# Seven products of sums of quarters for the last four output projections of an attention and feed-forward kernel

## The chip, the cores and the metric

One Trainium2 chip, one of its cores. The metric is the device time of one execution in microseconds (us); lower is better. The kernel before was run 13 times: median 1199.19 us, lowest 1196.18, highest 1206.77.

## The reference

Two blocks, one after the other, all in float32. The first is an attention in which each query and key is assigned to one of 16 clusters and a query sees only the keys of its own cluster. The second multiplies the result (3072 tokens by 512) by a 512 x 2048 matrix, gates it elementwise, and multiplies it by a 2048 x 512 matrix:

```
q, k, v: (4, 8, 768, 64);  centroids: (8, 16, 64);  w_in: (512, 2048);  w_out: (2048, 512)
mask   = argmax cluster of q == argmax cluster of k
attn   = softmax(where(mask, q k^T / 8, -1e9)) v
x      = attn as (4*768, 8*64)
h      = x @ w_in
g      = h * erf(softplus(h))
out    = g @ w_out
```

The change concerns the last line alone, out = g @ w_out.

## The kernel before

**Tiling.** The attention works on 16 pairs of heads (NPAIR), each pair in 12 units (two halves of 384 queries by six tiles of 128 keys). The feed-forward part works on 12 chunks of 256 tokens (TB), three for each batch. For one chunk `hidden(n)` (line 599) makes g's first factor: 8 groups of 8 matmuls, each with a 128x128 block of w_in as weights and 256 tokens as the moving operand, into a PSUM tile `hp` of one bank; VectorE copies each group into `gs[n]`. The `hp` tiles come from `ps_x` (line 103), a pool of four buffers that the attention's `av` and `psum` tiles use too. With the last group, `gate(n)` (line 567) queues two Softplus and two Erf activations on ScalarE and eight products on GpSimd (on VectorE for the last chunk). `project(n)` (line 623) makes the output: for each of the two tiles of 128 tokens, 16 matmuls over the 2048 hidden values, with g (128x128) as weights and all 512 columns of w_out moving, into a PSUM tile `po`; VectorE copies it to `osb`, and SyncE's queue writes it out in one DMA of 256 KB.

**fp32 in the profile.** Each float32 matmul of the code stands in the profile as two MATMUL instructions and two LDWEIGHTS: the 384 matmuls of all `project` calls are `po` x768, the 768 of `hidden` are `hp` x1536. All lines of engine work are shown as L61, the line of the helper `InOrder` that records them; the tile names tell them apart.

**Order.** `ffn_stream` (line 643) is one generator that yields a matmul at a time: `hidden(n)`, and, from the 17th matmul of `hidden(n)` on, two matmuls of `project(n-1)` behind each of its own (`i > 2 * GW * HP`, line 656). The loop over units at line 777 pumps this stream between the attention's matmuls. By its budget (line 791) the attention of the last batch ends when `hidden(8)` is through and `project(8)` has not begun. What is left then, beside no attention, is the loop of lines 802 to 807: the last six `attend` calls (`av`), the last `divide` (`psum`, then Ln and Exp on ScalarE, then `den`, `den` and two `xT` instructions on VectorE), and the rest of the stream: `hidden(9)`, `hidden(10)` and `hidden(11)` with `project(8)` to `project(11)`. Up to a slot of the first batch (`in_order`, lines 735 and 764) each engine's instructions are pinned to the order of the code. After that they are not: the framework orders each engine's instructions when the program is built, by the order of the code among those it takes to be ready, and an instruction can come to stand ahead of one that the code issues earlier.

**Tiles that the change takes over.** `prs` (line 124, eight tiles of 2 x 386 floats) holds exponentials that `attend` reads; `lows` (line 120) holds the routing rows that the second matmuls of `sc` read; `rowp` (`qT`, `kT`), `vp` (`in_v`), `accp` (`acc`) and `stage` (`in_q`, `in_k`) are operands of the attention; `ps_s` (line 102) has two buffers of two PSUM banks for the scores `sc`.

Of the kernel before, what the change touches and what calls it, by code (L numbers as in the profile page):

```python
# [9 lines left out]
F32 = mybir.dt.float32  # L10
# [4 lines left out]
ALU = mybir.AluOpType  # L15
# [4 lines left out]
P = 128  # L20
B, H, S, D = 4, 8, 768, 64
C = 16
NJ = S // P
Q = 32
NB = S // Q
HW = S // 2
HJ = NJ // 2
HP = H // 2
NPAIR = B * HP
DM, DFF = H * D, 2048  # L30
NFT = DFF // P
GW = 2
TB = 256
NCHUNK = B * S // TB
# [35 lines left out]
def kernel(  # L70
# [10 lines left out]
    nc = tc.nc  # L81

    in_order = [True]
    te, ve, ae, ge = (
        InOrder(tc, e, in_order) for e in (nc.tensor, nc.vector, nc.scalar, nc.gpsimd)
    )

    def pool(name, bufs, **kw):
        return ctx.enter_context(tc.tile_pool(name=name, bufs=bufs, **kw))

    const = pool("const", 1)
    stage = pool("stage", 1)
    vp = pool("vp", 2)
    rowp = pool("rowp", 2)
    routep = pool("routep", 1)
    small = pool("small", 2)
    accp = pool("accp", 2)
# [4 lines left out]
    ps_s = pool("ps_s", 2, space=PSUM)  # L102
# [10 lines left out]
    w_out = const.tile([P, NFT, DM], F32, name="w_out")  # L113
# [6 lines left out]
    lows = [  # L120
        {nm: const.tile([P, 2, S], BF16, name=f"{nm}m{i}") for nm in "qk"} for i in range(2)
    ]

    prs = [const.tile([P, 2, HW + 2], F32, name=f"pr{i}") for i in range(NPT)]
# [46 lines left out]
    for base, pattern, sign, op, fill in (  # L171
# [5 lines left out]
            out=first, in_=first, compare_op=op, fill=fill, base=base, pattern=pattern,  # L177
# [94 lines left out]
    for it in range(2):  # L272
# [4 lines left out]
            out=twice, in0=ss, scalar=inv, in1=norm, op0=ALU.mult, op1=ALU.add  # L277
# [3 lines left out]
            out=norm, in0=twice, scalar1=0.5, scalar2=(1e-6 if it else 0.0),  # L281
# [240 lines left out]
    def divide(u):  # L522

        p, half, _ = units[u]
        st = pairs[p]
        av = st["av", half]

        psum = ps_x.tile([P, HW], F32, name="psum", tag="x")
        for e in range(2):
            te.matmul(  # L530
                psum[e * D : (e + 1) * D], lhsT=minus, rhs=st["acc", half][:, e], start=True, stop=True
            )

        inv = routep.tile([P, HW], F32, name="inv")
        den = routep.tile([P, HW], F32, name="den")
        ae.activation(out=inv, in_=psum, func=ACT.Ln, bias=alleps, scale=-1.0)
        ae.activation(out=inv, in_=inv, func=ACT.Exp, scale=-1.0)
        yield
        ve.scalar_tensor_tensor(
            out=den, in0=psum, scalar=S * EPS, in1=inv, op0=ALU.subtract, op1=ALU.mult  # L540
        )
        ve.scalar_tensor_tensor(
            out=den, in0=den, scalar=2.0, in1=inv, op0=ALU.add, op1=ALU.mult
        )
        x = xTs.setdefault(p, {})
        lo = half * HW
        while lo < (half + 1) * HW:
            c = lo // TB
            hi = min((c + 1) * TB, (half + 1) * HW)
            if c not in x:  # L550
                x[c] = xTp.tile([P, TB], F32, name=f"xT{c}", bufs=XBUFS[c])
            mine = slice(lo - half * HW, hi - half * HW)
            ve.scalar_tensor_tensor(
                out=x[c][:, lo - c * TB : hi - c * TB], in0=av[:, mine], scalar=av[:, HW : HW + 1],
                in1=den[:, mine], op0=ALU.add, op1=ALU.mult,
            )
            lo = hi
        done.add((p, half))
        if half == 1:
            del pairs[p]  # L560
        yield


    TJ = TB // P
    CPB = S // TB
# [25 lines left out]
    def gate_products(n=NFT):  # L591
        for product in gating[:n]:
            product()
        del gating[:n]

    gs = {}
    resting = [0]

    def hidden(n):
        b, c = n // CPB, n % CPB  # L600
        gs[n] = gp.tile([P, NFT, TB], F32, name="g")
        for fp in range(NFT // GW):
            while converted[0] < DM // P * (fp * GW * P // LC + 1):
                yield None
            hp = ps_x.tile([P, GW, TB], F32, name="hp", tag="x")
            for a in range(GW):
                f0 = (fp * GW + a) * P
                for r in range(HP):
                    te.matmul(
                        hp[:, a], lhsT=w_in[:, r, f0 : f0 + P],  # L610
                        rhs=xTs[b * HP + r][c],
                        start=(r == 0), stop=(r == HP - 1),
                    )
                    if (a, r) != (GW - 1, HP - 1):
                        yield 4 * TB
            ve.tensor_copy(out=gs[n][:, fp * GW : (fp + 1) * GW], in_=hp)
            if fp == NFT // GW - 1:
                gate(n)
            yield 4 * TB

    out_v = out.rearrange("(b j p) m -> b j p m", p=P, j=NJ)

    def project(n):
        b, c = n // CPB, n % CPB
        gate_products()
        for tt in range(TJ):
            po = ps_x.tile([P, DM], F32, name="po", tag="x")
            for ft in range(NFT):
                while converted[0] < n_w_in + ft + 1:
                    yield None  # L630
                te.matmul(
                    po, lhsT=gs[n][:, ft, tt * P : (tt + 1) * P], rhs=w_out[:, ft],
                    start=(ft == 0), stop=(ft == NFT - 1),
                )
                if ft < NFT - 1:
                    yield 4 * DM
            osb = outp.tile([P, DM], F32, name="osb")
            ve.tensor_copy(out=osb, in_=po)
            nc.sync.dma_start(out=out_v[b, c * TJ + tt], in_=osb)
            yield 4 * DM  # L640
        del gs[n]

    def ffn_stream():


        late = iter(())
        for n in range(NCHUNK):
            b, c = n // CPB, n % CPB
            halves = range(c * TB // HW, ((c + 1) * TB - 1) // HW + 1)
            while not all((b * HP + r, h) in done for r in range(HP) for h in halves):  # L650
                yield None
            i = 0
            for cost in hidden(n):
                yield cost
                i += cost is not None
                if n > 1 and i > 2 * GW * HP:
                    for _ in range(2):
                        if (x := next(late, None)) is not None:
                            yield x
            yield from late  # L660
            late = project(n)
        yield from late

    stream = ffn_stream()
    pumped = [0]

# [35 lines left out]
    for e in range(2):  # L702
        ve.tensor_copy(
            out=ccT[e * D : (e + 1) * D, :, e * C : (e + 1) * C],
            in_=pct[e * D : (e + 1) * D].rearrange("d (r e c) -> d r e c", e=2, c=C)[:, :, e],
# [11 lines left out]
    for e in range(2):  # L717
        ve.reduce_sum(
            out=own[:, e : e + 1],
            in_=ident.rearrange("p (g x c) -> p x g c", x=2, c=C)[:, e], axis=AX.XY,  # L720
# [13 lines left out]
    for slot in range(2 * NJ * HP):  # L734
        in_order[0] = slot < FIRST
        p, r = divmod(slot, 2 * NJ)
# [40 lines left out]
    for u in range(2 * NJ * HP, len(units), 2):  # L777
        p, half, j = units[u]
# [24 lines left out]
        attend(n)  # L803
    for _ in divide(len(units) - 1):
        pass
    while next(stream, None) is not None:
        pass

# [31 lines left out]
```

## Time and profile before

| what | value |
|---|---|
| median of 13 runs | 1199.19 us |
| the profiled execution: its time, its span | 1197.19 us, 1195.5 us |
| TensorE (PE) busy, whole span | 1147.6 us, 96% |
| VectorE (DVE), ScalarE (ACT), GpSimd (POOL) busy | 516.4, 587.0, 462.0 us |
| last matmul of the attention (`psum`) done, by the chain | 998.9 us |
| `hidden(9)` begins, last matmul of `project(11)` done | 998.9 us, 1191.85 us |
| one fp32 matmul of `hidden` (two instructions), in a stretch of 49 (98 instructions) | 0.432 us |
| one fp32 matmul of `project` (two instructions), in a stretch of 32 (64 instructions) | 0.859 us |
| DMA landing of an output tile | 2.0 us, median |
| granted TensorE clock, whole span, and from 998.8 us on | 0.986, 1.00 |

The span is from the first instruction to the last; the profiled execution's time is 1.69 us above it. A matmul's own duration in the profile (0.597 us for `po`) holds its latency, and matmuls overlap; what one costs in a stream is the distance from start to start, which the table gives. "Idle before" is time in which an engine stood still ahead of an instruction, with the instruction that ended the wait.

### The profile page before, as it was taken

To read this page: it belongs to the slowest core of one execution; us is meant where nothing else is said; L and a number is where in the kernel's file an instruction comes from. 1 tells how busy PE (TensorE), PEld (TensorE's weight loads), DVE (VectorE), ACT (ScalarE), POOL (GpSimd) and SP (SyncE) were. 2 spreads that over 40 slices of the span, in tenths; PEclk is the share of its full clock that TensorE was granted. 3 is DMA by queue.
4 is the path that set the end of the run, shared out by engine and by line. 5 is a ranking of instruction groups with operands and counts; after the bars stand their busy time and mean duration, and the time that the engine had idled before them with its cause. 6 is when DMAs were issued, how large, how long until landed. Compare 5 with 4: busy or idle time off the path is not lost.

```text
span 1195.5 us, 13349 instructions
## 1 busy us (share of the span) xinstructions
PE 1147.6 (96%) x4912; PEld 618.9 (52%) x4912; DVE 516.4 (43%) x971; ACT 587.0 (49%) x682; POOL 462.0 (39%) x466
## 2 busy tenths in 40 slices
PE   4999979899999989999999999999999999999998
PEld 1333356554544555564474446465456456576663
DVE  7788785635443544343452434434354012111121
ACT  5888896863525372462553454164355253222221
POOL 3677764553333433261453243144234253031100
PEclk8999989999999989999999999999999999999999
DMA  8652442110201010020201101020000000000000
GB/s 137 169 124 41 111 147 53 54 27 23 45 13 27 23 27 22 9 40 1 45 14 18 41 8 34 9 36 14 10 23 1 9 9 1 18 1 18 9 9 18
DMA packets 140561, 42.95 MB, mean 36 GB/s; under 512 B 133328, under 2 KB 133328, under 8 KB 140496
## 3 DMA queue, kind: packets, MB, share of 16 engines
q1 hardware_dynamic: 137360, 41.70, 15.4%
q10 hardware_dynamic: 3136, 0.39, 0.3%
q8 instruction: 39, 0.64, 0.2%
q14 instruction: 26, 0.21, 0.1%
HBM read 35.68 MB, written 6.29 MB: 35 GB/s over the span
## 4 chain that ended last, share of the span: by engine, by line
PE 78%; ACT 8%; issue 7%; DVE 4%; DMA 2%; POOL 1%; ACTq 0%; SPq 0%; DVEq 0%
PE po L61 25%; PE hp L61 25%; PE sc L61 13%; PE av L61 8%; PE sm L61 4%; ACT km L61 2%; ACT w_out L61 2%; ACT L61 2%; PE psim L61 1%; DVE nmx L61 1%; ACT pr L61 1%; PE psum L61 1%; ACT inv L61 1%; DVE den L61 1%; ACT a_s L61 1%
## 5 line engine op out<-in xcount | busy, mean ns | idle before, releaser
L61 PE MATMUL hp<-xT,w_in 128*128 128x256 f32 x1536 | 385.8, 388 | 8.0 <-DVE xT L61 6.3
L61 PE MATMUL po<-w_out,g 128*128 128x512 f32 x768 | 367.9, 597 | 0.6 <-DVE den L61 0.6
L61 PEld LDWEIGHTS hp<-xT,w_in 128*128 128x128 f32 x1536 | 288.3, 192 | 128.2 <-issue 83.6
L61 POOL TENSOR_TENSOR acc<-acc,pr 128x384 f32<-128x384 f32 x256 | 236.6, 954 | 292.9 <-ACT pr L61 292.7
L61 DVE TENSOR_REDUCE nmx<-sm 128x1 f32<-128x384 f32 x384 | 195.8, 550 | 142.3 <-PE sm L61 141.4
L61 ACT ACT_TABLE_LOAD x110 | 141.1, 1283 | 231.9 <-DVE g L61 128.9
L61 ACT ACTIVATE pr<-sc 128x768 f32<-128x768 f32 x192 | 146.9, 806 | 146.8 <-PE sc L61 146.6
L61 PEld LDWEIGHTS po<-w_out,g 128*128 128x128 f32 x768 | 142.0, 190 | 106.8 <-issue 94.0
L61 POOL TENSOR_TENSOR g<-a_s,g 128x512 f32<-128x512 f32 x88 | 111.5, 1299 | 216.6 <-ACT a_s L61 216.6
L61 PE MATMUL sc<-qT,kT 64*128 64x384 f32 x768 | 181.7, 529 | 4.8 <-ACT pr L61 4.7
L61 DVE COPY g<-hp 128x512 f32<-128x512 f32 x96 | 66.0, 687 | 255.0 <-PE hp L61 254.7
L61 PE MATMUL av<-pr,in_v 128*64 128x386 f32 x768 | 140.0, 496 | 0.0
L61 PE MATMUL sm<-km,qm 128*128 128x384 bf16 x384 | 103.1, 337 | 16.4 <-DVE nmx L61 6.4
L61 PEld LDWEIGHTS sc<-qT,kT 64*128 64x128 f32 x768 | 70.1, 189 | 82.1 <-issue 47.5
L61 POOL TENSOR_TENSOR acc<-pr,pr 128x384 f32<-128x384 f32 x64 | 65.3, 1040 | 89.7 <-ACT pr L61 89.5
L61 PEld LDWEIGHTS av<-pr,in_v 128*64 128x64 f32 x768 | 49.2, 136 | 80.9 <-issue 70.5
L61 PEld LDWEIGHTS <-qm 128*128 128x128 bf16 x384 | 34.8, 99 | 83.1 <-issue 68.5
L61 DVE SCALAR_TENSOR_TENSOR den<-psum,inv 128x384 f32<-128x384 f32 x32 | 17.8, 557 | 129.2 <-ACT inv L61 128.8
L61 ACT ACTIVATE w_out<-w_out 128x512 int32<-128x512 uint32 (+2 forms) x68 | 61.9, 953 | 2.2 <-DMA w_out<-in_moe_w_out_dram 1.6
L61 ACT ACTIVATE a_s<-g 128x2048 f32<-128x2048 f32 x24 | 45.9, 1910 | 32.5 <-DVE g L61 32.4
L61 PE MATMUL sc<-qm,km 64*128 64x384 bf16 x384 | 59.1, 327 | 0.1
L61 ACT ACTIVATE a_s<-a_s 128x2048 f32<-128x2048 f32 (+2 forms) x32 | 53.9, 1686 | 0.4
(75 smaller groups left out, 560.5 us busy)
## 6 DMA issues: line engine op xcount, KB each, us to landing
w_out<-in_moe_w_in_dram SPq DMA_DIRECT2D x16, 512.0 KB, 6.6
in_q<-in_q_dram SPq DMA_DIRECT2D x64, 96.0 KB, 3.0
in_v<-in_v_dram SPq DMA_DIRECT2D x32, 192.0 KB, 2.9
w_out<-in_moe_w_out_dram SPq DMA_DIRECT2D x12, 512.0 KB, 3.3
out_dram<-osb SPq DMA_DIRECT2D x24, 256.0 KB, 2.0
in_k<-in_k_dram SPq DMA_DIRECT2D x60, 96.0 KB, 3.4
qm<-nmT SPq DMA_DIRECT2D x186, 0.2 KB, 1.7
a_s<-in_moe_w_out_dram SPq DMA_DIRECT2D x4, 512.0 KB, 3.3
```

The lines of the kernel that those rows point to most:

```text
L61: ins = getattr(self.engine, name)(*args, **kw)
```

## The change

`project` stays for chunks 0 to 7. Chunks 8 to 11 (`FAST` is 8) go through `project_fast`. It takes g of a chunk as 2 x 2 quarters (two token tiles by two halves of the hidden values, eight tiles of 128 each) and w_out as 2 x 2 quarters (two halves of the hidden values by two halves of 256 columns), and forms the four quarters of the output from seven products of sums of quarters instead of eight products of quarters. A product is eight matmuls of 256 moving columns. The sums of w_out (`add_weights`, 24 adds of 128x256, every fourth on GpSimd) and the differences, made in place (`subtract_weights`, 8 instructions of 128x512), are made once, behind the last `divide`; the sums of g (`add_hidden`: six adds, of 768 or 256 elements a partition, and two in-place differences of 1024) once per chunk. All sums lie in tiles that the attention no longer needs. The products go to two `ps_s` tiles, four quarters of 256 columns in each; VectorE puts the output together in two `stage` tiles with two copies and eight adds or subtracts of 256 columns, and four DMAs of 128 KB write it out. In `ffn_stream` the `hidden` of chunks 9, 10 and 11 is no longer mixed with the projection of the chunk before: all 64 matmuls of `hidden(n)` come first, then all of `project_fast(n-1)`. `project_fast` does not call `gate_products` itself.

```diff
+    FAST = NCHUNK - CPB - 1
+    HF, HM = NFT // 2, DM // 2
+
+    def g_part(n, tt, fh):
+        return gs[n][:, fh * HF : (fh + 1) * HF, tt * P : (tt + 1) * P]
+
+    def w_part(fh, mh):
+        return w_out[:, fh * HF : (fh + 1) * HF, mh * HM : (mh + 1) * HM]
+
+    w_sum = {}
+    g_sum = {}
+
+    def add_weights():
+
+        planes = [t[:, e, 0:HM] for t in prs for e in range(2)]
+        planes += [
+            t[nm].bitcast(F32)[:, e, 0:HM] for t in lows for nm in "qk" for e in range(2)
+        ]
+        for name, (x, y) in {"++": ((0, 0), (1, 1)), "0+": ((0, 0), (0, 1)), "1+": ((1, 0), (1, 1))}.items():
+            w_sum[name] = [planes.pop(0) for _ in range(HF)]
+            for f in range(HF):
+                (ge if f % 4 == 3 else ve).tensor_tensor(
+                    out=w_sum[name][f], in0=w_part(*x)[:, f], in1=w_part(*y)[:, f], op=ALU.add
+                )
+
+    def subtract_weights():
+
+        for x, y in (((0, 1), (1, 1)), ((1, 0), (0, 0))):
+            for f in range(0, HF, 2):
+                ve.tensor_tensor(
+                    out=w_part(*x)[:, f : f + 2], in0=w_part(*x)[:, f : f + 2],
+                    in1=w_part(*y)[:, f : f + 2], op=ALU.subtract,
+                )
+
+    def add_hidden(n):
+        if n % 2:
+            tiles = [rowp.tile([P, S], F32, name=nm + "T") for nm in "qkqk"]
+        else:
+            tiles = [vp.tile([P, NJ, 2, D], F32, name="in_v") for _ in range(2)]
+            tiles = [t.rearrange("p j e d -> p (j e d)") for t in tiles]
+            tiles += [
+                accp.tile([P, 2, HW], F32, name="acc").rearrange("p e n -> p (e n)") for _ in range(2)
+            ]
+        tiles = [t.rearrange("p (f t) -> p f t", t=P) for t in tiles]
+        lot = S // P
+        sums = g_sum[n] = {}
+        for i, (name, x, y) in enumerate(
+            (("+1", (1, 0), (1, 1)), ("0+", (0, 0), (0, 1)), ("++", (0, 0), (1, 1)))
+        ):
+            rest = slice(i * (HF - lot), (i + 1) * (HF - lot))
+            sums[name] = [tiles[i][:, f] for f in range(lot)] + [tiles[3][:, f] for f in range(rest.start, rest.stop)]
+            for fs, o in ((slice(0, lot), tiles[i]), (slice(lot, HF), tiles[3][:, rest])):
+                ve.tensor_tensor(out=o, in0=g_part(n, *x)[:, fs], in1=g_part(n, *y)[:, fs], op=ALU.add)
+        for x, y in (((1, 0), (0, 0)), ((0, 1), (1, 1))):
+            ve.tensor_tensor(out=g_part(n, *x), in0=g_part(n, *x), in1=g_part(n, *y), op=ALU.subtract)
+
+    def project_fast(n):
+        b, c = n // CPB, n % CPB
+        add_hidden(n)
+        gsum = g_sum[n]
+        one = ps_s.tile([P, 2, 512], F32, name="sc", tag="s").rearrange("p e (h m) -> p (e h) m", h=2)
+        two = ps_s.tile([P, 2, 512], F32, name="sc", tag="s").rearrange("p e (h m) -> p (e h) m", h=2)
+        osb = [
+            stage.tile([P, NB, Q], F32, name="in_" + nm).rearrange("p n t -> p (n t)")[:, 0:DM] for nm in "qk"
+        ]
+
+        def product(o, g, w):
+            for f in range(HF):
+                te.matmul(
+                    o, lhsT=g[f] if isinstance(g, list) else g[:, f],
+                    rhs=w[f] if isinstance(w, list) else w[:, f], start=(f == 0), stop=(f == HF - 1),
+                )
+                yield 4 * HM
+
+        def put(tt, mh, x, y, op):
+            ve.tensor_tensor(out=osb[tt][:, mh * HM : (mh + 1) * HM], in0=x, in1=y, op=op)
+
+        def so_far(tt, mh):
+            return osb[tt][:, mh * HM : (mh + 1) * HM]
+
+        m3, m4, m2, m5 = (one[:, i] for i in range(4))
+        m6, m7, m1 = (two[:, i] for i in (0, 1, 2))
+        yield from product(m3, g_part(n, 0, 0), w_part(0, 1))
+        yield from product(m4, g_part(n, 1, 1), w_part(1, 0))
+        yield from product(m2, gsum["+1"], w_part(0, 0))
+        yield from product(m5, gsum["0+"], w_part(1, 1))
+        ve.tensor_copy(out=so_far(0, 1), in_=m3)
+        ve.tensor_copy(out=so_far(0, 0), in_=m4)
+        put(1, 0, so_far(0, 0), m2, ALU.add)
+        put(1, 1, so_far(0, 1), m2, ALU.subtract)
+        put(0, 1, so_far(0, 1), m5, ALU.add)
+        put(0, 0, so_far(0, 0), m5, ALU.subtract)
+        for tt in range(TJ):
+            nc.sync.dma_start(
+                out=out_v[b, c * TJ + tt, :, (1 - tt) * HM : (2 - tt) * HM], in_=so_far(tt, 1 - tt)
+            )
+        yield from product(m6, g_part(n, 1, 0), w_sum["0+"])
+        yield from product(m7, g_part(n, 0, 1), w_sum["1+"])
+        put(1, 1, so_far(1, 1), m6, ALU.add)
+        put(0, 0, so_far(0, 0), m7, ALU.add)
+        yield from product(m1, gsum["++"], w_sum["++"])
+        for tt in range(TJ):
+            put(tt, tt, so_far(tt, tt), m1, ALU.add)
+            nc.sync.dma_start(
+                out=out_v[b, c * TJ + tt, :, tt * HM : (tt + 1) * HM], in_=so_far(tt, tt)
+            )
+        del gs[n]
+
     def ffn_stream():
 
 
@@ -653,12 +764,12 @@
             for cost in hidden(n):
                 yield cost
                 i += cost is not None
-                if n > 1 and i > 2 * GW * HP:
+                if 1 < n <= FAST and i > 2 * GW * HP:
                     for _ in range(2):
                         if (x := next(late, None)) is not None:
                             yield x
             yield from late
-            late = project(n)
+            late = (project if n < FAST else project_fast)(n)
         yield from late
 
     stream = ffn_stream()
@@ -803,6 +914,8 @@
         attend(n)
     for _ in divide(len(units) - 1):
         pass
+    add_weights()
+    subtract_weights()
     while next(stream, None) is not None:
         pass
 
```

## The prediction

> **What bounds the kernel now.** I read the page's slices first, then the chain of waits, then the stage that the change touches. In the slices (tenths of busy time in 40 slices) the last seven, from about 986 us on, are the stage beside no attention:
>
> ```profile
> PE   4999979899999989999999999999999999999998
> DVE  7788785635443544343452434434354012111121
> POOL 3677764553333433261453243144234253031100
> PEclk8999989999999989999999999999999999999999
> ```
>
> TensorE is full there, at full clock, and VectorE and GpSimd are nearly empty. The busy time of each engine from 998.8 us to the last matmul says it in one line: 193.03 of 193.10 us on TensorE, 28.68 on VectorE.
>
> ```profile
> core 0: us, PE busy (x) PEld busy (x) DVE busy (x) ACT busy (x) POOL busy (x), PEclk, DMA share, GB/s
> 998.80:1191.90 193.10, 193.03 (x642) 121.68 (x640) 28.68 (x44) 43.65 (x29) 24.69 (x20) 1.00 0.03 10
> ```
>
> The chain that ended last is TensorE alone there; two pieces of it give the prices (start, length, work, instructions):
>
> ```profile
> 1040.37 21.15 PE hp L61 x98
> ...
> 1164.37 27.48 PE po L61 x64
> 1191.85 0.02 issue
> 1191.87 0.69 DVE osb L61
> ```
>
> So a fp32 matmul (two instructions) with 256 moving columns costs 2 x 21.15 / 98 = 0.4316 us, one with 512 columns 2 x 27.48 / 64 = 0.8588 us. Check: from 998.89 (first `hp` of chunk 9 in the chain) to 1191.85 are 192.96 us; 192 matmuls of `hidden` by 0.4316 and 128 of `project` by 0.8588 make 82.9 + 109.9 = 192.8. Fewer matmul columns here shorten the kernel one for one, until TensorE has to wait.
>
> The place where it may have to wait is the hand-over from the attention. VectorE there (start, length, work, idle before):
>
> ```profile
> 994.61 0.68 DVE L61 COPY g<-hp 128x512 f32<-128x512 f32 x1
> 995.21 0.74 DVE L61 SCALAR_TENSOR_TENSOR xT<-av,den 128x256 f32<-128x256 f32 x2
> 1002.64 0.69 DVE L61 COPY g<-hp 128x512 f32<-128x512 f32 x1 [6.69 <-PE hp L61]
> 1004.22 0.56 DVE L61 SCALAR_TENSOR_TENSOR den<-psum,inv 128x384 f32<-128x384 f32 x1 [0.89 <-ACT inv L61]
> 1004.81 1.08 DVE L61 SCALAR_TENSOR_TENSOR den<-den,inv 128x384 f32<-128x384 f32 x1
> 1005.93 0.75 DVE L61 SCALAR_TENSOR_TENSOR xT<-av,den 128x128 f32<-128x128 f32 x2
> ```
>
> and GpSimd:
>
> ```profile
> 972.46 4.95 POOL L61 TENSOR_TENSOR g<-a_s,g 128x512 f32<-128x512 f32 x4 [4.26 <-ACT a_s L61]
> ...
> 989.52 3.60 POOL L61 TENSOR_TENSOR acc<-acc,pr 128x384 f32<-128x384 f32 x4 [2.52 <-ACT pr L61]
> 1000.54 4.94 POOL L61 TENSOR_TENSOR g<-a_s,g 128x512 f32<-128x512 f32 x4 [7.42 <-ACT a_s L61]
> ```
>
> VectorE has a hole of 6.69 us ahead of chunk 9's first copy. And the gating at 972.46 runs ahead of accumulations that the code issues before it (it is chunk 8's first half, issued with the attention's last pump or later): instructions without a pin move forward to where they are ready. That decides where the new sums go.
>
> [...] `den<-den,inv` takes 559 ns in the median, and 1.08 us at 1004.81, where the gating runs. [...]
>
> **The products (gain).** Per chunk 32 matmuls of 512 columns, 27.48 us, become 7 x 8 = 56 of 256 columns, 56 x 0.4316 = 24.17 us. The row is `hp`: same type, same weights (128x128), same 256 columns, new weights each time; [...] and the upper bound is the rival on loads below. Gain 3.31 us a chunk, four chunks: **13.25 us**. That `hidden` and projection are no longer mixed changes no sum on TensorE: the `hp` stretch of 98 ran unmixed at its price.
>
> **Sums of w_out (once).** VectorE 18 adds x 0.424 = 7.6 us and 8 differences x 0.687 = 5.5 us, 13.1 in all; GpSimd 6 adds of 256: from 954 ns (384) and 1268 (512) an estimate of 0.64 each, 3.8 us. They are wanted by the first product at about 998.9 + 64 x 0.4316 = 1026.5 us, so the sums themselves are in time. What they can delay is what stands behind them on VectorE: chunk 9's first copy and the last `den` and `xT`. TensorE has four `ps_x` buffers, `av` and `psum` hold two until 1006.7, so `hp` groups 0 and 1 (8 x 0.4316 = 3.45 us each) fill the others, and group 2 wants one back at 998.9 + 6.9 = 1005.8. Four "++" adds (from `prs` 0 and 1, last read by the `av` matmuls at 975 to 979), the eight "1+" adds (`lows`, last read at 988.6) and the four differences of (1,0) can go into the idle time before 994. From 996 on remain 9 adds and 4 differences on VectorE, 3.8 + 2.7 = 6.6 us, against the hole of 6.69: 1002.6, just when the copy is due. [...] 3 adds on GpSimd and its gating from 1000.54, up to 6.9 us of GpSimd in the same time. If a third to a half of this lands on VectorE, the copy ends at 1006 to 1007.5. I take **1.5 us** of stall; bounds 0 (it all fits; a gain is excluded, since TensorE has no idle time to win there) and 8.6 (rival 1).
>
> **Sums of g (per chunk).** 3 x (0.957 + 0.424) + 2 x 1.224 = 6.6 us of VectorE; with 4.7 us for two copies (0.42) and eight adds (0.48, from `xT` 128x256 with 483 ns) and 5.5 us of copies it has 17 us of work in 51.7 us of TensorE. Cost 0: for chunks 8 to 10 a whole `hidden` of 27.6 us or a projection of 24.2 us lies between the end of `gate(n)` and the first product; for chunk 11, 24.2 us of `project_fast(10)` cover what the trace of before shows from the last copy (1164.4) to the last product of the gate (1174.1), 9.7 us, and 6.6 us of sums: 16.3. If that cover were gone, the first two products (6.9 us) read no sum of g and cover the rest. Each `hidden` needs a copy every 3.45 us; a sum ahead of it lasts at most 1.22 us, and there are four buffers. The leftover gating of chunk 8, issued now with `gate(9)`, is ready where it was and goes forward as before: 0.
>
> **PSUM, stages, DMAs.** `one` of the next chunk wants a buffer that was read 10 us before; the stage tiles wait for DMAs of 2 us with 6.9 us to go. SP's queue has 16 DMAs in place of 8 and is otherwise empty: 0 but for the end. There two adds of 0.48 take the place of one copy of 0.69, [...]: **+0.3 us** (0 to 0.6).
>
> **Sum.** 1197.19 - 13.25 + 1.5 + 0.3 = 1185.7 us against the profiled execution. That one is 2.0 us below the median of the runs shown, so 1187.7 against the median, 11.5 less or 1.0%. Own range 1184.5 (no stall, and a median nearer the lowest run) to 1190.5.
>
> **Rivals.**
> 1. The sums of w_out do not move forward, and all stand ahead of the first copy: 998.2 + 13.1 + 2.4 (`den`, `xT`) + 0.7 = 1014.4 against 1005.8, a stall of 8.6 us: 1194.8 against the median. For it: they are issued ahead of `hidden(9)`, so they come first where all are ready. Against it: the gating at 972.46.
> 2. Slower. The sums of chunk 8 too stand ahead of the first copy, [...]: 13.1 + 6.6 of VectorE, 3.8 + 4.9 of GpSimd, 2.4 + 0.7, from 994.6: 1026. Stall 20 us, sum +7: 1206. It decides from a first copy at 1005.8 + 13 = 1019 on, and is over the bound from 1022. Against it: the copies come before those sums in the code.
> 3. The product is not as cheap as its columns: loads per chunk rise from 64 to 112 instructions at 190 ns, 21.3 of 24.2 us. If 26 ns of each of 448 showed, 11.7 us of the gain would be gone: 1199.4. Against it: the `hp` stretch.
>
> **Chances.** A measurement of this kernel can tell about 0.3% (3.6 us) from no change. Likeliest case 0.71 and rival 1 0.16, both faster by more; rival 2 0.07; rival 3 0.06, within. Faster 0.87, same 0.06, slower 0.07. The range takes in rival 1 with its end at 0.6 and leaves out 2 and 3: 1184.5 to 1195.5.
>
> **What would show it.** Products in the chain at 0.432 us each, 56 a chunk, 24.2 us; `hp` without a break for 27.6 us; from the end of `psum` to the last matmul 181 us. A wait of `hp` on VectorE near 1006 is the stall; over 8 us is rival 1, over 13 rival 2; more such waits, or waits of the products on sums of g, would be a step that I costed at nothing. A spacing above 216 ns in the products is rival 3.

## The result and the profile after

The changed kernel takes 1188.74 us (median of 11 runs, 1182.89 to 1190.32), the kernel before 1198.71 us (median of 48 runs, those shown ahead of the prediction among them). The ratio, taken of the means, is **0.9911, 95% interval 0.9892 to 0.9930**: about 10.7 us less, with an interval from 8 to 13 us (the medians are 10.0 us apart). The prediction was 11.5 us less, 0.9904, and 1187.7 us.

The profiled execution took 1183.35 us, with a span of 1181.6 us: 13.9 us below that of before. Not all of this is the change: chunk 9 begins at 996.02 us instead of 998.82, and in the profiled executions told of below it begins anywhere from 996 to 1009 us, though the edits hardly touch what lies ahead. So I compare the **stretch**: from the start of the first `hp` matmul of chunk 9 (behind the last `psum`) to the end of the last matmul. Before it is 193.03 us, after 996.02 to 1178.07, **182.05 us: 10.98 less**. Each stretch is read from one profiled execution of its kernel. How well it repeats is seen from e4 and e12 below, two variants with the same waits: 182.04 and 182.05 us.

The slices of the page after, to be held against those of before: VectorE now works at the end, and TensorE is as full as it was.

```profile
PE   4999979899999989999999999999999999999998
DVE  7788885536443544334363345334345216442351
POOL 3677873645333424152344243335134346213000
```

Busy time of each engine in the stretch: VectorE's rises from 28.68 to 70.31 us (sums, differences, and the adds that put the output together, `put` in the code), weight loads (PEld) from 121.68 to 157.90, and TensorE is idle for under 2 of 182 us.

```profile
core 0: us, PE busy (x) PEld busy (x) DVE busy (x) ACT busy (x) POOL busy (x), PEclk, DMA share, GB/s
996.00:1178.10 182.10, 180.39 (x834) 157.90 (x832) 70.31 (x115) 43.65 (x29) 26.96 (x21) 1.00 0.03 11
```

The chain that ended last. The products appear as `sc`, the name of the tile that they are written to:

```profile
998.26 5.10 DVE w_out L61 x3
1003.36 0.61 DVE g L61
1003.97 0.04 issue
1004.01 20.99 PE hp L61 x96
1025.00 20.72 PE sc L61 x96
1045.72 1.29 PE hp L61 x6
1047.02 3.45 PE sc L61 x16
...
1173.53 0.42 DVE in_k L61
1173.95 0.34 DVE in_q L61
1174.30 0.04 issue
1174.34 3.73 PE sc L61 x16
```

Three things are to be seen. The products cost what the `hp` row promised: 96 instructions in 20.72 us, 0.4317 us a matmul. From the start of chunk 9 on the chain leaves TensorE at two places, which are its two waits: the differences of w_out ahead of the first copy of chunk 9, and two adds of the output ahead of the last eight matmuls (TensorE idle for 0.84 us). And between the sixth and the seventh product of chunk 8 stand three `hp` matmuls (six instructions) of chunk 10, a sign that the seventh product has something to wait for there too.

The hand-over on VectorE and, in the last fence, on GpSimd (start, length, work, idle before):

```profile
993.07 4.66 DVE L61 TENSOR_TENSOR pr<-w_out 128x256 f32<-128x256 f32 x9
997.66 5.70 DVE L61 TENSOR_TENSOR w_out<-w_out 128x512 f32<-128x512 f32 x4
1003.28 0.68 DVE L61 COPY g<-hp 128x512 f32<-128x512 f32 x1
```

```profile
997.74 6.74 POOL L61 TENSOR_TENSOR g<-a_s,g 128x512 f32<-128x512 f32 x4 [1.29 <-ACT a_s L61]
```

Exactly nine adds and four differences are left for the hole behind the attention, as the prediction counted. But the four differences take 5.70 us, not 2.7, and the four gating products on GpSimd beside them 6.74 us where they took 4.94 before. The first copy starts at 1003.28; TensorE, which has filled two buffers by 1003.0, goes on at 1004.01. Its third group is about 1.1 us late.

### The profile page after: what moved, and what is told of

The parts are those of the page before. It is cut to its first block, busy times and chain, and to the rows that moved or that the text cites. A ratio compares the mean times of both kernels' runs of the same rounds, so it can differ in the third digit from the quotient of the medians.

```text
span 1181.6 us, 13871 instructions
## 1 busy us (share of the span) xinstructions
PE 1131.3 (96%) x5104; PEld 652.6 (55%) x5104; DVE 567.8 (48%) x1061; ACT 587.3 (50%) x682; POOL 470.1 (40%) x472
## 4 chain that ended last, share of the span: by engine, by line
PE 75%; ACT 8%; issue 7%; DVE 6%; DMA 2%; POOL 1%; SPq 0%; DVEq 0%; ACTq 0%
PE hp L61 24%; PE sc L61 21%; PE po L61 16%; PE av L61 7%; PE sm L61 4%; ACT w_out L61 2%; ACT L61 2%; DVE nmx L61 2%; ACT km L61 1%; PE psim L61 1%; ACT pr L61 1%; PE psum L61 1%; DMA in_q<-in_q_dram 1%; ACT inv L61 1%; DVE den L61 1%
## 5 line engine op out<-in xcount | busy, mean ns | idle before, releaser
L61 PE MATMUL hp<-xT,w_in 128*128 128x256 f32 x1536 | 376.2, 386 | 9.1 <-DVE xT L61 6.2
L61 PE MATMUL po<-w_out,g 128*128 128x512 f32 x512 | 250.1, 599 | 0.6 <-DVE den L61 0.6
L61 PEld LDWEIGHTS po<-w_out,g 128*128 128x128 f32 x512 | 93.3, 190 | 66.6 <-issue 56.5
L61 ACT COPY nmT<-pn 6x128 bf16<-6x128 bf16 x31 | 7.7, 249 | 93.9 <-PE pn L61 93.9
```

The lines of the kernel that those rows point to most:

```text
L61: ins = getattr(self.engine, name)(*args, **kw)
```

## The experiments

**The theory.** The gain is the difference of matmul columns, 3.31 us a chunk. It loses about 1.1 us at the third group of chunk 9, where differences of w_out, slowed by GpSimd's gating, stand ahead of a copy, and 0.84 us at the last product; the sums of g cost nothing. **The rivals:** the sums fit anywhere, so nothing depends on their place (against the first); the waits merely swap (if one goes, another comes); and part of the gain or loss lies in the new order, products behind and not mixed.

### The sums held in the place of the code (e1)

```diff
+    in_order[0] = True
     add_weights()
     subtract_weights()
+    for _ in range(2 * GW * HP):
+        next(stream)
+    in_order[0] = False
```

> The sums of w_out and the first two groups of the hidden product of chunk 9 are pinned to the order of the code, so that no sum of w_out moves ahead of the last division and the first two copies stand behind all of them. My theory: the change keeps its gain only because most of these sums run in idle VectorE time before the hand-over; pinned, the first copy of chunk 9 comes 14 to 18 us later than in the changed kernel, TensorE stands still for 13 to 17 us at its third group, and the time is 1.003 (1.001 to 1.006) of the kernel before instead of 0.991. The rival, that VectorE has room enough wherever the sums stand: at most 2 us more than the changed kernel, 0.993 or less.

Measured: 0.9988 (0.9960 to 1.0016), stretch 189.29 us, 7.2 more than the changed kernel. TensorE at the hand-over:

```profile
998.59 7.17 PE L61 MATMUL hp<-xT,w_in 128*128 128x256 f32 x32
1006.93 7.17 PE L61 MATMUL hp<-xT,w_in 128*128 128x256 f32 x32 [1.17 <-DVE den L61]
1015.90 5.02 PE L61 MATMUL sc<-w_out,g 128*128 128x256 f32 x22 [1.79 <-DVE w_out L61]
1020.75 14.04 PE L61 MATMUL hp<-xT,w_in 128*128 128x256 f32 x64
```

The first copy comes at 1019.98, as late as expected, but TensorE loses only about 3.6 us by it (1.17 and 1.79 us idle, and the restarts): `den` and `xT`, ahead of the sums, free two PSUM buffers, so that four groups run; and from 1015.90 on TensorE takes 11 matmuls of chunk 8's products while it has no buffer for `hp`. The wait at the end follows as in the changed kernel. The largest loss, some 4.8 us, is at the seventh product of chunk 8: it waits 3.09 us for VectorE at 1055.58 and then takes 5.13 us for 16 instructions that need 3.45 elsewhere. VectorE is late there because a sum of chunk 9's g, which stands ahead of the copies and adds of chunk 8's output, waits for GpSimd's gating until 1045.85; and ahead of 1004.07 it stood idle for 8.34 us in the same way, with a sum of chunk 8's g first in line. So the place of the sums decides most of the gain, against the rival, but my size for it was twice too large (7.2 us instead of 13 to 17), and the larger part of the loss came at a place that I had not thought of.

### Without the sums of w_out, without the sums of g (e3, e4)

```diff
-    add_weights()
-    subtract_weights()
+    for name, (fh, mh) in {"++": (0, 0), "0+": (0, 1), "1+": (1, 1)}.items():
+        w_sum[name] = w_part(fh, mh)
```

> Leaves out the sums and differences of w_out: the products use plain quarters of w_out in the same shapes, so the output is not the reference's. My theory: they cost only the wait of 0.8 us at the third group of chunk 9 and some 0.3 us at the last copy of chunk 8; without them both waits are gone and the time is 1 us below the changed kernel, about 0.990 of the kernel before. The rival, [...]: 3 us or more below the changed kernel, 0.988 or less.

Measured: 0.9900 (0.9868 to 0.9932), stretch 180.12 us, 1.9 less. The wait at the third group is gone. Some 0.9 us of the 1.9 is work that moved: without differences to wait for, two matmuls of the first product (four `sc` instructions, 0.93 us at 991.75) go ahead of the stretch. What the sums cost is then 1.0 us, and not the 3 us or more of the rival.

```diff
-        add_hidden(n)
-        gsum = g_sum[n]
+        gsum = {"+1": g_part(n, 1, 0), "0+": g_part(n, 0, 1), "++": g_part(n, 0, 0)}
```

> Leaves out the sums and differences of g in all four chunks: the products use plain quarters of g in the same shapes, so the output is not the reference's. My theory: 26 us of VectorE work lie wholly beside TensorE, so the time is that of the changed kernel within 1 us, 0.991 of the kernel before. The rival, that they hold up copies or products: 2 us or more below it, 0.989 or less.

Measured: 0.9902 (0.9874 to 0.9929), stretch 182.04 us against 182.05. The sums and differences of g, 28.6 us of VectorE's busy time in the changed kernel, cost nothing.

### Two chunks instead of four (e7)

```diff
-    FAST = NCHUNK - CPB - 1
+    FAST = NCHUNK - 2
...
             yield from late
+            if n == FAST:
+                add_weights()
+                subtract_weights()
...
-    add_weights()
-    subtract_weights()
```

> Only chunks 10 and 11 go by seven products; chunks 8 and 9 are projected and mixed as in the kernel before, and the sums and differences of w_out come behind the projection of chunk 9. My theory: the gain is 3.31 us for each chunk, so 6.6 less 0.84 for the wait ahead of the last product: the stretch from the first matmul of chunk 9 is 187.2 us (193.03 before, 182.05 with four chunks), the time 0.995 of the kernel before. The rival, that a fixed part of the gain comes from the order (no mixing) or from the attention's end: more than 7 or less than 4 us of gain.

Measured: 0.9965 (0.9938 to 0.9993), stretch 187.55 us, a gain of 5.48 where 5.8 was expected; the wait ahead of the last product costs 1.1 us and not 0.84, as e6 below shows, and with that added back it is 6.6. The other two chunks bring 187.55 - 182.05 = 5.5, with the 1.1 at the third group, which e7 does not have, 6.6 too. So the gain goes by chunks, 3.3 us each, and no fixed part of it comes from the order.

### The products mixed with the next chunk's hidden product (e5, e11, e12)

```diff
-                if 1 < n <= FAST and i > 2 * GW * HP:
+                if n > 1 and i > 2 * GW * HP:
```

> The products of chunk n-1 are mixed with the hidden product of chunk n from its 17th matmul on, two for one, as in the kernel before, instead of coming behind all 64. My theory: the sum of TensorE work is the same and VectorE has its sums ready in time, so only the wait at the third group stays, 0.991 of the kernel before, within 1.5 us of the changed kernel. The rival, that putting the products behind is what gives the sums their time: the first product of chunk 8 waits for its differences and sums from about 1003 us on, 3 to 8 us more, 0.994 to 0.998.

Measured: 0.9961 (0.9940 to 0.9982), stretch 188.73 us. In this version the sums of chunk 8 are issued ahead of part of chunk 8's gating, so they are sums of a g that is not finished. Next, that was mended, and then the last chunk left unmixed:

```diff
+        gate_products()
         add_hidden(n)
...
-                if 1 < n <= FAST and i > 2 * GW * HP:
+                if n > 1 and i > 2 * GW * HP:
+                if 1 < n < NCHUNK - 1 and i > 2 * GW * HP:
```

The first of the two conditions is that of e11, the second that of e12.

> The products of chunk n-1 mixed with the hidden product of chunk n from its 17th matmul on, as in e5_mixed, but with the gating of chunk n-1 issued ahead of its sums, so that the result is the reference's (e5_mixed took the sums of chunk 8 from a g whose gating was not all issued). My theory from e5_mixed: the loss is not at chunk 8 but at the end, where no projection of chunk 10 is left to cover the 9.7 us from the last hidden matmul of chunk 11 to its gated g: a wait of 4.6 us ahead of the second product of chunk 11 and some 2 us within it, the stretch from the first matmul of chunk 9 is 188 to 190 us instead of 182.05. The rival, that the early sums of chunk 8 in e5_mixed made the loss: 183 us or less.

> As e11_mixed_gated, but the products of chunk 10 come behind all of the hidden product of chunk 11, as in the changed kernel; only chunks 8 and 9 are mixed. My theory: being behind is worth something for the last chunk alone, so the stretch is 182 us within 0.5, as in the changed kernel, 0.991 of the kernel before. The rival, that mixing costs at each chunk: a third of the loss of e11_mixed_gated goes and two thirds stay, 186 us or more.

Measured: e11 0.9965 (0.9945 to 0.9985), stretch 188.56 us; e12 0.9878 (0.9843 to 0.9913), stretch **182.05 us**, that of the changed kernel to the hundredth. The size of e5's rival was right and its place wrong. The loss lies at the end of e11:

```profile
1163.59 3.62 PE L61 MATMUL sc<-w_out,g 128*128 128x256 f32 x16
1163.79 0.69 DVE L61 COPY g<-hp 128x512 f32<-128x512 f32 x1 [2.76 <-PE hp L61]
...
1169.08 1.91 ACT L61 ACTIVATE a_s<-a_s 128x2048 f32<-128x2048 f32 x1
1171.02 2.50 DVE L61 TENSOR_TENSOR g<-a_s,g 128x512 f32<-128x512 f32 x4 [6.53 <-ACT a_s L61]
1171.76 5.41 PE L61 MATMUL sc<-w_out,g 128*128 128x256 f32 x16 [4.55 <-DVE g L61]
```

The first product of chunk 11 reads the early half of g and runs at once, for 3.5 us; the second reads the late half, whose copy, table loads, activations and gating take from 1163.8 to 1173.5. TensorE waits 4.55 us. Its next 16 instructions then take 5.41 us instead of 3.62, but not by further waits, as I had expected: the profile has none among them. The clock that TensorE is granted, 1.00 from 1163 to 1167, is 0.50 for about 3 us (the last column but two):

```profile
1172.20:1175.40 3.20, 3.20 (x9) 2.51 (x8) 3.20 (x6) 0.00 (x0) 0.00 (x0) 0.50 0.02 5
```

The same is seen in e1 behind its wait of 3.09 us (a clock of 0.52 from 1055.60 to 1058.60) and in e5 behind one of 4.56 us (0.50 from 1172 to 1178), and behind none of the shorter waits, of up to 1.79 us. In the changed kernel the 24 us of chunk 10's products lie between the last copy of chunk 11 and its products. Being behind is worth 6.5 us for the last chunk (4.8 of wait and restart, 1.7 of the lower clock) and nothing for the others.

### The last product in a tile of its own (e6)

```diff
-        m6, m7, m1 = (two[:, i] for i in (0, 1, 2))
+        m6, m7 = (two[:, i] for i in (0, 1))
...
+        m1 = ps_x.tile([P, HM], F32, name="m1", tag="x")
         yield from product(m1, gsum["++"], w_sum["++"])
```

> The product of the diagonal sums goes to a PSUM tile of its own instead of the second bank of the tile of the two products before it. My theory: the wait of 0.84 us ahead of the last 8 matmuls of the kernel is a wait for the reads of that shared tile, and is gone; the three matmuls of the next chunk that stand in its place in chunks 8 to 10 go behind. The stretch from the first matmul of chunk 9 falls from 182.05 to 181.2 us, 0.990 of the kernel before. The rival, that it waits for a sum or for the stage tiles: the wait of 0.84 us stays.

Measured: 0.9903 (0.9877 to 0.9929), stretch 180.95 us, 1.1 less. No wait is left at the end:

```profile
1153.52 20.72 PE sc L61 x96
1174.24 3.47 PE m L61 x16
```

So the seventh product waited for VectorE's reads of the two before it, which it does not need, because the three share a tile of two banks; the sums and the stage tiles, which the rival named, are as before. The wait costs 1.1 us, more than the 0.84 that TensorE is idle: the last 16 instructions take 3.47 us here and 3.73 behind the wait.

### The sums of w_out spread (e2, e8), the last differences behind the copies (e9)

e2 issues the 32 sums and differences four at a time behind the eight copies of chunk 9 and pins them there (`add_weights` and `subtract_weights` now yield behind each instruction); e8 is e2 and e6 together:

```diff
+                yield
...
-    add_weights()
-    subtract_weights()
+    sums = (x for part in (add_weights(), subtract_weights()) for x in part)
+    for _ in range(NFT // GW):
+        for _ in range(GW * HP):
+            next(stream)
+        in_order[0] = True
+        for _ in range(4):
+            next(sums, None)
+        in_order[0] = False
```

> The sums and differences of w_out are issued four at a time behind each of the eight copies of chunk 9 and pinned there, so that none stands ahead of a copy in a lump. My theory: the wait of some 1.1 us at the third group and the 0.3 us at the last copy of chunk 8 are gone; from the first matmul of chunk 9 to the last of all 180.4 to 181.0 us instead of 182.05 in the changed kernel, and the time 1 to 1.5 us below it, about 0.990 of the kernel before. The rival, that VectorE's work there only moves its wait: the first products of chunk 8 wait for the last differences, and the stretch stays at 182 or grows.

> Both edits together: the sums of w_out spread behind the copies of chunk 9, and the last product in a tile of its own. My theory: the two waits are separate, so both go: the stretch from the first matmul of chunk 9 is 179.7 to 180.2 us against the bare sum of 416 matmuls by 0.4316, 179.55, and the time is 2 to 2.5 us below the changed kernel, 0.989 of the kernel before. The rival: one wait takes the place of the other, and the stretch is 181 us or more.

Measured: e2 0.9917 (0.9895 to 0.9940), stretch 183.27 us, 1.2 more; e8 0.9936 (0.9909 to 0.9964), stretch 181.14 us, no better than e6 alone. The rival won both. `hp` indeed runs on, 112 instructions in 24.39 us, but now the last differences come when the first products want them (waits of the products on `w_out`, 0.7 us): in e2 four of these differences take 5.96 us beside the gating of chunk 9 on GpSimd, and the four behind it 2.48. And in e2 the seventh product makes TensorE wait twice.

e9 keeps e6's tile, lets all sums go forward, and pins only the four differences that overwrite what the last adds read, one behind each of the first four copies:

```diff
-        for x, y in (((0, 1), (1, 1)), ((1, 0), (0, 0))):
+        for x, y in (((1, 0), (0, 0)), ((0, 1), (1, 1))):
             for f in range(0, HF, 2):
+                if x == (0, 1):
+                    for _ in range(GW * HP):
+                        next(stream)
+                    in_order[0] = True
...
+                in_order[0] = False
```

> Last product in its own tile as in e6_own_bank, and of the sums of w_out only the last four differences are pinned, one behind each of the first four copies of chunk 9; all others go forward as in the changed kernel. My theory: what holds the first copy back is these four differences alone; the wait of 1.1 us at the third group goes and nothing takes its place, the stretch is 179.7 to 180.1 us instead of 180.95, 0.989 of the kernel before. The rival, as e2_sums_spread and e8_spread_own_bank went: another wait takes its place, 180.9 us or more.

Measured: 0.9897 (0.9860 to 0.9935), stretch **179.86 us**, 2.2 less than the changed kernel and 0.3 above the bare sum of 416 matmuls (179.55). `hp` runs from 1009.05 without a wait:

```profile
1009.05 21.20 PE L61 MATMUL hp<-xT,w_in 128*128 128x256 f32 x97
```

The stretch is the shortest of all. In the times of whole executions 2 us less cannot be told from the changed kernel; the intervals overlap.

### GpSimd taken away from the differences (e10)

```diff
-                    (ge if n < NCHUNK - 1 else ve).tensor_tensor, out=h[:, i : i + GW],
+                    (ge if n < NCHUNK - 1 and n != FAST else ve).tensor_tensor, out=h[:, i : i + GW],
```

> The changed kernel with the eight gating products of chunk 8 on VectorE instead of GpSimd, so that GpSimd reads nothing while the last four differences of w_out run. My theory: [...] without GpSimd beside them they take 2.5 us, the first copy of chunk 9 comes 2 to 3 us earlier against the end of psum, and the wait at the third group is gone though VectorE has 2.7 us more to do; stretch 181.0 us instead of 182.05. The rival, that the differences are slow of themselves or wait for something else: 5.7 us again and the same wait or a longer one.

Measured: 0.9903 (0.9872 to 0.9934), stretch 180.97 us, 1.1 less. VectorE:

```profile
999.22 4.65 DVE L61 TENSOR_TENSOR pr<-w_out 128x256 f32<-128x256 f32 x9
1003.80 2.48 DVE L61 TENSOR_TENSOR w_out<-w_out 128x512 f32<-128x512 f32 x4
1006.20 0.68 DVE L61 TENSOR_TENSOR g<-a_s,g 128x512 f32<-128x512 f32 x1
```

The same nine adds take the same 4.65 us, and the same four differences 2.48 us instead of 5.70, with no gating on GpSimd beside them. So it is the gating beside them that makes these four slow (it takes longer there too, 6.74 us against 4.94 in the kernel before), and the cause of the wait at the third group is shown. It takes both: the wait is gone when GpSimd is not beside the differences (here), and when the differences stand behind the copies (e9).

## Why the prediction was right, step by step

- **The products, 13.25 us.** Right. The price of 0.4316 us was met (0.4317), and e7 shows the gain for each pair of chunks. Rival 3, dearer loads, is out: with 112 loads a chunk, of 190 ns each in the mean (those of `hp` take as long), the products keep the spacing of `hp`, 0.216 us an instruction.
- **The sums of w_out, 1.5 us.** Right in kind and nearly in size: 1.1 us at the third group, and 0.33 us ahead of the last group of chunk 8, where sums that moved forward delay a copy (TensorE's idle time there is 1.11 us, before 0.78). The second was taken for free. The count of what is left for the hole was exact. That VectorE is slower beside GpSimd's work is shown by e10: 3.2 us more on the four differences, where the prediction took a third to a half of 6.9, my estimate, with one instruction of before behind it (`den<-den,inv` at 1004.81, 0.52 us over its median). The prices themselves were met: an add of 256 columns, put at 0.424 us, which the trace of before does not show, takes 0.41 to 0.42 in the median of the trace after, and a difference of 512, put at 0.687 (the mean of VectorE's gating products in before), 0.68 with no gating beside it (e10).
- **The sums of g, 0.** Right (e4). Their prices of 0.957 us for 768 columns and 1.224 for 1024, not shown by the trace of before either, are near those of the trace after: 0.94 to 0.96 and 1.21 to 1.23 us, with 1.42 to 2.01 for the three of 768 that begin beside GpSimd's gating. But the sentence on what it costs if their cover is gone was wrong. I wrote that the first two products read no sum and cover the rest, and forgot that the second reads the half of g that is gated last. With the cover gone (e11) the cost is 6.5 us. And they are free only in this order: in e1 VectorE waits in front of such sums while other work stands behind them.
- **PSUM, 0.** Wrong by 1.1 us (e6): I looked at the next chunk's buffers only, and took two banks of one tile for independent. In chunks 8 to 10 three matmuls of the next chunk fill the wait; behind chunk 11 there are none.
- **The end, +0.3.** Two adds of 0.42 us, not 0.48; and the transfers of 128 KB, which the prediction put at the 2.0 us of those of 256 KB, land in 1.7 to 1.8 us in the median. From the last matmul to the end of the span are 3.53 us, before 3.65: -0.1.
- **The sum.** 13.25 - 1.1 - 1.1 = 11.05 in the stretch, where 10.98 were measured; less 0.33 ahead of it, and 0.1 more at the end, 10.8, against 11.5 predicted and 10.7 measured. That the whole came so near is in part luck: 1.4 us that the prediction had at nothing were lost, and its stall and its end were each 0.4 us too dear. The interval of the ratio, 8 to 13 us, could not tell these parts; they are read from the traces.
- **Rivals 1 and 2.** e1 brings their case about. The stretch is 7.2 us longer than in the changed kernel, which is rival 1's number (8.6 instead of 1.5), but by another path: the hand-over costs 3.6 us and the seventh product of chunk 8 4.8. Their working let TensorE stand still from its third group on, though `den` and `xT` free two buffers first and other matmuls are ready. Rival 2's 20 us, for which the work of VectorE and of GpSimd was added up, did not come.

Open: why chunk 9 begins at 996 us in one execution and at 1009 in another. TensorE's mean granted clock goes with it in most: it is 0.989 and 0.990 in the two profiled executions that begin first (996.02 in the changed kernel, 996.76 in e6) and 0.976 to 0.980 in the four that begin last (1006.14 to 1009.05, e2, e5, e9 and e11). What sets it is not shown here, and no verdict on the stretch rests on it.

## What to carry to other kernels

Where one engine is full, price a change by what the same instruction costs in that engine's own stream, and take the difference. Then look, wherever one stage hands over to the next, for the instruction that stands last ahead of a buffer's release, and, if it is a two-input instruction of VectorE, ask what GpSimd does at that moment (here 5.70 us beside its gating, 2.48 without). Fewer products need sums, and the sums need time: put the products where other matmuls lie between them and the making of their operands, the last chunk above all. Give an accumulator that comes late a tile of its own.

## What the runs showed of the hardware

- Four 128x512 differences on VectorE, both inputs in SBUF, took 2.48 us with no gating beside them (e10) and 5.70 us beside four 128x512 products on GpSimd, which took 6.74 us instead of 4.94 (before). That is not far from one after the other (2.48 + 4.94 = 7.42). VectorE's copy out of PSUM took its usual time: 0.68 us at 1003.28, beside the last of the same products.
- The fp32 matmuls of 256 columns, with new weights each time, stood 0.216 us an instruction apart, `hp` and products alike, and mixing the two changed nothing: e12 and the changed kernel have the same 182.05 us.
- The waits of TensorE cost more here than their idle time: an idle time of 0.82 or 0.84 us made the stretch 1.1 us longer (e10, e6). Behind waits of 3.09, 4.55 and 4.56 us (e1, e11, e5) the granted clock was about 0.5 for 3 to 6 us; behind waits of up to 1.79 us it was not.
